# Turning the keys of batches 1 to 3 on VectorE, from loads in 16 pieces

## The chip, the cores and the metric

The kernel runs on one core of a Trainium2 chip. The metric is the device time of one execution in microseconds (us), median of several runs. A separate profiled execution gives the durations that are quoted here.

## The reference

Two blocks, one after the other. The first is a linear attention with a polynomial sketch of features; the second is a two-layer perceptron with exact Gelu on its output.

```python
batch, n_heads, seq, head_dim = (4, 4, 1088, 32); r = 8
def phi(x):                                  # S1, S2: (8, 32)
    a = np.einsum('rd,bhsd->bhsr', S1, x)
    b = np.einsum('rd,bhsd->bhsr', S2, x)
    return np.einsum('bhsi,bhsj->bhsij', a, b).reshape(*x.shape[:-1], r * r)
q_p, k_p = (phi(q), phi(k))
kv = np.einsum('bhsf,bhsd->bhfd', k_p, v)
z = np.sum(k_p, axis=2)
num = np.einsum('bhsf,bhfd->bhsd', q_p, kv)
den = np.einsum('bhsf,bhf->bhs', q_p, z)[..., None] + 1e-06
attn = num / den                             # -> x: (4352, 128), heads side by side
h = x @ w_in                                 # (4352, 2048)
g = 0.5 * h * (1.0 + erf(h / sqrt(2)))
out = g @ w_out                              # (4352, 128)
```

S1, S2, w_in and w_out arrive as 64-bit floats and are rounded to 32 bits on the chip.

## The kernel before, in words

Of the 1088 tokens of a batch, 1024 are "main" and 64 "remainder". The main tokens of the four batches make eight chunks of 512, and the remainders of all four make a ninth of 256. For each chunk n and each of 16 slices fi of the hidden width, `hidden(n, fi)` multiplies x (transposed, in xT) by a 128x128 block of w_in (L466), ScalarE applies Gelu (L468), and `project(n, fi)` adds the product with a block of w_out into o_ps (L481, L478 for the last chunk). These 144 steps are TensorE's main work. Step t runs hidden(t), then what was put in slot t, then project(t - 2). Chunks 0 and 1 share the first 32 steps, and chunks 2 and 3, of batch 1, follow from step 32.

The attention of later batches is put in slots between these steps. For batch b, with t the first step of its first chunk (32, 64, 96):

- slot t-20: `widen_v` and `widen_v_rem` copy v on GpSimd into v_aug and v_rem_aug, beside columns of ones (L278, L286).
- slot t-18: the keys are turned, so that the 32 head dimensions lie on partitions. `turn_keys` calls `key_turn(b, r, work_bank(), by_dve)` for r = 0, 1, each with four 128x128 TensorE transposes into a PSUM bank (in `transposed`, L265), and VectorE copies the bank to kT (L267).
- slot t-17: `features` calls `key_features`: 32 small matmuls per r against the sketches S12 (L303), ScalarE copies of one factor (L316), VectorE products (L317) into k_p.
- slots t-16 and t-15, for batch 1 only: `key_turn_rem` and `key_features_rem` do the same for the remainders of batches 1 and 3 (k_rem, kT_rem, k_p_rem).
- slot t-14: `finish_keys` sums k_p times v_aug over the tokens (`kv_sum`, L336; `kv_sum_rem`, L343) and takes the sum out. Slot t-13 turns that 128x128 result (L352).
- slots t-13, t-12, t-8 of each chunk: queries turned on VectorE (`query_turn`, L367), expanded (L376, L397), attended (L417, L424, L428), giving xT.

In slots 4 to 21 the rest of the weights is rounded, on VectorE and ScalarE (L209 to L239). Batch 0 is done ahead of the steps, with TensorE transposes of its own.

Which token lies where is set by the load. `load_main` (L95) puts token p*8 + j of each head on partition p at place j, in one transfer per tensor and batch with runs of 1 KB. Since kv sums over all tokens, any order will do for k and v as long as k_p and v_aug meet with the same token. `load_q` (L105) loads the queries of later chunks in four pieces of 32 partitions per chunk, so that VectorE's block transposes give the wanted order. All loads and most stores are issued by SP in the order of the text. `load_rest` issues, after the first part, the rest of the weights, then for b = 1, 2, 3 the keys, values and queries, with the remainders (k_rem, v_rem, L108) after batch 1's queries, and q_rem at the end.

The instructions of each engine run in the order of the text; a loop at the end of the kernel pins that order. PSUM tiles w_ps come from the pool wps, which has two buffers; kT has two buffers.

Of the kernel before, what the change touches and what calls it, by code (L numbers as in the profile page):

```python
# [8 lines left out]
FP = mybir.dt.float32  # L9
# [7 lines left out]
def kernel(  # L17
# [18 lines left out]
    pe, dve, act, pool, sp = nc.tensor, nc.vector, nc.scalar, nc.gpsimd, nc.sync  # L36
    B, H, S, D = q.shape
# [7 lines left out]
    MAIN = J * 128  # L45
    REM = S - MAIN
    JC = 4
    CW = JC * 128
# [9 lines left out]
    att = ctx.enter_context(tc.tile_pool(name="att", bufs=2))  # L58
# [5 lines left out]
    def work_banks():  # L64

        return wps.tile([128, 2, CW], FP, name="w_ps")

    def work_bank():
        return work_banks()[:, 0]
# [11 lines left out]
    by_act, by_dve, by_pool = act.copy, dve.tensor_copy, pool.tensor_copy  # L81
# [5 lines left out]
    main = {(n, b): big.tile([128, H, J, D], FP, name=f"{n}_{b}") for n in "kv" for b in range(B)}  # L87
# [6 lines left out]
    def load_main(eng, n, b, heads=slice(0, H)):  # L94
        eng.dma_start(out=main[n, b][:, heads],  # L95
                      in_=src_of[n][b, heads, 0:MAIN, :].rearrange("h (p j) d -> p h j d", j=J))

    def load_q(n):
        at = n % NCH * CW
        if n < NCH:  # L100
            sp.dma_start(out=q_sb[n], in_=q[0, :, at:at + CW, :].rearrange("h (p j) d -> p h j d", j=JC))
            return
        src = q[n // NCH, :, at:at + CW, :].rearrange("h (t g j) d -> g t h (j d)", g=G, j=JC)
        for g in range(G):
            sp.dma_start(out=q_sb[n][g * 32:(g + 1) * 32].rearrange("t h j d -> t h (j d)"), in_=src[g])  # L105

    def load_rem(n, b):
        sp.dma_start(out=rem[n][b // 2 * REM:(b // 2 + 1) * REM, b % 2],  # L108
                     in_=src_of[n][b, :, MAIN:S, :].rearrange("h p d -> p h d"))
# [12 lines left out]
    def load_w_in(i, gated=False):  # L122
        src, e = words(moe_w_in)
        c0, c1 = pieces[i]
        to = landing(w_in_sb[i], e == 2)
        if gated:

            pool.memset(to[0:1, 0:1], 0)
        sp.dma_start(out=to, in_=src[:, c0 * e:c1 * e])

    def load_w_out(i):
        src, e = words(moe_w_out)
        sp.dma_start(
            out=landing(w_out_sb[i], e == 2).rearrange("p (fo d) -> p fo d", d=d_model * e),
            in_=src[slice(*pieces[i]), :].rearrange("(fo fi) d -> fi fo d", fi=128))

    S_dst = landing(SR, S1.dtype != FP)
    for i, s in enumerate((S1, S2)):
        s, e = words(s)
        act.dma_start(out=S_dst[i * R:(i + 1) * R, :].rearrange("r (h d) -> r h d", h=H),  # L140
                      in_=s[:, None, :].broadcast_to([R, H, e * D]))
    nc.scalar.preload_act_table_set("gelu_and_others")
    for r in range(2):
        load_main(sp, "k", 0, slice(r, H, 2))
    load_q(0)
    load_main(sp, "v", 0)
    load_rem("k", 0)
    load_rem("k", 2)
    load_w_in(0)
    load_rem("v", 0)  # L150
    load_q(1)
    load_w_in(1)
    load_w_out(0)
    load_w_out(1)

    def load_rest():

        for i in range(2, len(pieces)):
            load_w_in(i, gated=i == 2)
            load_w_out(i)  # L160
        for b in range(1, B):
            for n in "kv":
                load_main(sp, n, b)
            for c in range(NCH):
                load_q(b * NCH + c)
            if b == 1:
                for n, b1 in (("k", 1), ("k", 3), ("v", 1), ("v", 2), ("v", 3)):
                    load_rem(n, b1)
        for b in range(B):
            load_rem("q", b)  # L170
# [90 lines left out]
    def transposed(ps, name, srcs, copy):  # L261

        n = len(srcs) * 128
        for i, s in enumerate(srcs):
            pe.transpose(ps[:, i * 128:(i + 1) * 128], in_=s, identity=ident)  # L265
        t = att.tile([128, CW], FP, name=name, bufs=3 if name == "xT" else 2)
        copy(out=t[:, :n], in_=ps[:, :n])  # L267
        return t

    def four_tokens(n, b, h, c):  # L270
        return main[n, b][:, h, c * JC:(c + 1) * JC, :].rearrange("p j d -> p (j d)")


    kT, k_p, k_p_rem, kv_T = {}, {}, {}, {}
# [13 lines left out]
    def key_turn(b, r, ps, copy):  # L288
        kT[r] = transposed(ps, "kT", [four_tokens("k", b, h, c) for h in (r, r + 2) for c in range(NCH)], copy)

    def spread(out, a, b):

        n = a.shape[1]
        return dict(out=out, in0=a[:, :, :, None].broadcast_to([128, n, R, R]),
                    in1=b[:, :, None, :].broadcast_to([128, n, R, R]))

    def key_features(b, r, banks, by_pool=()):

        for i in range(2 * NCH):
            for c in range(2):  # L300
                for t in range(2):
                    at = i * 128 + c * 64
                    pe.matmul(banks[t][c * 64:(c + 1) * 64, i * 32:(i + 1) * 32],  # L303
                              lhsT=kT[r][t * 64:(t + 1) * 64, at:at + 64],
                              rhs=S12[t * 64:(t + 1) * 64, 2 * t:2 * t + 2].rearrange("p h r -> p (h r)"),
                              start=True, stop=True)

        k_p[b, r] = att.tile([128, 2, J, R, R], FP, name="k_p")
        a = att.tile([128, 2, J, 2 * R], FP, name="a_t")
        for t in (1, 0):  # L310
            ab = banks[t][:, :128].rearrange("p (n r) -> p n r", r=2 * R)
            if t in by_pool:
                act.copy(out=a[:, t], in_=ab)
                pool.tensor_mul(**spread(k_p[b, r][:, t], a[:, t, :, 0:R], a[:, t, :, R:2 * R]))
            else:
                act.copy(out=a[:, t, :, 0:R], in_=ab[:, :, 0:R])  # L316
                dve.tensor_mul(**spread(k_p[b, r][:, t], a[:, t, :, 0:R], ab[:, :, R:2 * R]))  # L317
# [5 lines left out]
    def key_features_rem(pair, ps):  # L323
        pe.matmul(ps[:, 384:448], lhsT=kT["rem"][:, :128], rhs=S12.rearrange("p h r -> p (h r)"), start=True, stop=True)
        k_p_rem[pair] = big.tile([128, H, R, R], FP, name=f"k_p_rem{pair}")
        ab = ps[:, 384:448].rearrange("p (h r) -> p h r", r=2 * R)
        a = att.tile([128, H, R], FP, name="a_rem")
        act.copy(out=a, in_=ab[:, :, 0:R])
        dve.tensor_mul(**spread(k_p_rem[pair], a, ab[:, :, R:2 * R]))

    def kv_sum(b, ps, r):

        for i in range(J):
            ch, t, one = i // 4, i // 2 % 2, i % 2
            for c in range(NP):
                pe.matmul(ps[c * 64:(c + 1) * 64, r * F:(r + 1) * F], lhsT=v_aug[:, 2 * c + r, i, :],  # L336
                          rhs=k_p[b, r][:, t, c * 4 + ch * 2 + one].rearrange("p i j -> p (i j)"),
                          start=(r == 0 and i == 0), stop=False, skip_group_check=True)
# [12 lines left out]
    def turn_kv(b, ps, copy):  # L351
        pe.transpose(ps[:, :128], in_=kv_T[b], identity=ident)  # L352
        copy(out=kz[b].rearrange("p c n -> p (c n)"), in_=ps[:, :128])
# [158 lines left out]
    r = Rounding(SR)  # L512
# [20 lines left out]
    expand_multiply(0, 0)  # L533
    kv_bank = out_bank()
    kv_sum(0, kv_bank, 0)
    expand_copy(0, 2)
    key_features_rem(0, banks[1])
    expand_copy(0, 3)
    expand_multiply(0, 1)
    kv_sum(0, kv_bank, 1)  # L540
    kv_sum_rem(0, kv_bank)
    w_in[0].exponents()
# [7 lines left out]
    w_in[0].low_words()  # L550
    w_in[0].mantissas(by_pool=True)
    load_rest()
    w_in[0].product(pool)
    w_in[1].low_words()
# [26 lines left out]
    def at(t, f, *a):  # L581
        slots[t].append(lambda: f(*a))

    def turn_keys(b, r):
        key_turn(b, r, work_bank(), by_dve)

    def features(b, r):
        key_features(b, r, halves(work_banks()))
# [10 lines left out]
    def finish_keys(b):  # L599
        held["kv"] = work_bank()  # L600
        for r in range(2):
            kv_sum(b, held["kv"], r)
        kv_sum_rem(b, held["kv"])
        take_kv(b, held["kv"], by_dve)
# [15 lines left out]
    for b in range(1, B):  # L620
        t = NCH * b * NF
        for r in range(2):
            at(t - 20, widen_v, b, r)
        at(t - 20, widen_v_rem, b)
        for r in range(2):
            at(t - 18, turn_keys, b, r)
        for r in range(2):
            at(t - 17, features, b, r)
        if b == 1:
            at(t - 16, turn_keys_rem, b)  # L630
            at(t - 15, features_rem, b)
        at(t - 14, finish_keys, b)
        at(t - 13, lambda b=b: turn_kv(b, held["kv"], by_dve))
    for n in range(2, NCHUNK):
        t = n * NF
# [59 lines left out]
```

## Time and profile before

| | |
|---|---|
| median of 11 runs | 294.17 us (293.59 to 296.1) |
| the profiled execution | 293.96 us, span 291.6 us |
| PE (TensorE) busy | 282.3 us (97%) |
| DVE (VectorE) busy | 120.7 us (41%) |
| ACT (ScalarE) busy | 135.1 us (46%) |
| POOL (GpSimd) busy | 15.1 us (5%) |
| DMA packets | 32561, 13.37 MB |

The span is the time from the first to the last profiled instruction. The chain that ended last is followed back from the last instruction, at each step to what released it, so its shares add up to the span. PE is a matmul and PEld the load of its weights, which overlaps other matmuls; neighbouring matmuls overlap as well, so the durations of a row add up to more than the time that they take. Step 14 begins at 45.1 us, and step 32 is chunk 2's first.

### The profile page before, as it was taken

What the parts mean: (1) busy time and instruction counts of PE and PEld (TensorE: products, weight loads), DVE (VectorE), ACT (ScalarE), POOL (GpSimd) and SP (SyncE); (2) the same over time, 40 slices, a digit from 0 to 9 for tenths busy, and PEclk for the clock granted to TensorE, in tenths of its full rate; (3) what the DMA queues carried; (4) which work ended last, traced back from release to release, by engine and by line L of the source; (5) the groups of instructions that cost most, each with busy time, mean ns of one, the idle gap of its engine ahead of it and who ended that gap; (6) DMA issues with size and microseconds to landing.
All of it is one profiled execution on the core that took longest, in us unless ns stands there. A gap on an engine that the chain in (4) does not pass through costs nothing.

```text
span 291.6 us, 3792 instructions
## 1 busy us (share of the span) xinstructions
PE 282.3 (97%) x1497; PEld 137.1 (47%) x1497; DVE 120.7 (41%) x186; ACT 135.1 (46%) x259; POOL 15.1 (5%) x45
## 2 busy tenths in 40 slices
PE   7887999999999999999999999999999999999994
PEld 5633445643443345543443345533443344444694
DVE  6985686343813184251713085242513161221000
ACT  4673774265435442265335533256336533443341
POOL 3340200200000000300000000000000000000000
PEclk9999999999999999999999999999999999999999
DMA  7569587000012000200002000200001000200010
GB/s 217 160 203 370 102 231 215 7 0 0 2 28 34 11 0 2 36 2 0 0 0 37 0 2 0 39 0 0 0 9 29 0 0 0 36 2 0 9 29 18
DMA packets 32561, 13.37 MB, mean 46 GB/s; under 512 B 21408, under 2 KB 31904, under 8 KB 32544
## 3 DMA queue, kind: packets, MB, share of 16 engines
q1 hardware_dynamic: 32304, 13.05, 17.4%
q8 instruction: 12, 0.20, 0.2%
q10 hardware_dynamic: 240, 0.08, 0.1%
q14 instruction: 5, 0.04, 0.0%
HBM read 10.90 MB, written 2.23 MB: 45 GB/s over the span
## 4 chain that ended last, share of the span: by engine, by line
PE 91%; DVE 5%; issue 1%; ACT 1%; DMA 1%; ACTq 0%; DVEq 0%
PE h_ps L466 39%; PE o_ps L481 38%; PE o_ps L478 2%; PE w_ps L376 2%; PE w_ps L417 2%; PE w_ps L336 2%; DVE q_pT L397 1%; PE w_ps L265 1%; PE w_ps L303 1%; DMA raw_SR<-in_S_dram 1%; DVE k_p L317 1%; DVE bits_a L215 1%; DVE bits_e L234 0%; DVE bits_m L229 0%; PE h_ps L442 0%
## 5 line engine op out<-in xcount | busy, mean ns | idle before, releaser
L468 ACT ACTIVATE g<-h_ps 128x512 f32<-128x512 f32 (+1 forms) x144 | 82.5, 574 | 130.2 <-PE h_ps L466 129.9
L466 PE MATMUL h_ps<-xT,w_in 128*128 128x512 f32 (+1 forms) x288 | 140.3, 569 | 1.5 <-POOL w_in L239 0.8
L481 PE MATMUL o_ps<-g,w_out 128*128 128x512 f32 x256 | 133.1, 601 | 0.2 <-POOL w_out L239 0.2
L466 PEld LDWEIGHTS h_ps<-xT,w_in 128*128 128x128 f32 x288 | 53.5, 190 | 63.9 <-issue 60.3
L481 PEld LDWEIGHTS o_ps<-g,w_out 128*128 128x128 f32 x256 | 46.2, 190 | 58.1 <-issue 56.5
L424 DVE RECIPROCAL den<-den 128x512 f32<-128x512 f32 (+1 forms) x7 | 21.9, 3124 | 44.1 <-ACT den L423 44.1
L397 DVE TENSOR_TENSOR q_pT<-A_sb,w_ps 64x512 f32<-64x512 f32 x32 | 22.1, 691 | 25.4 <-ACT A_sb L383 24.8
L491 DVE STREAM_TRANSPOSE oT<-o_ps 128x512 f32<-128x512 f32 x8 | 5.7, 717 | 43.9 <-PE o_ps L481 43.9
L383 ACT COPY A_sb<-w_ps 64x512 f32<-64x512 f32 (+1 forms) x36 | 17.7, 556 | 3.1 <-PE w_ps L376 3.0
L428 DVE TENSOR_TENSOR xT<-w_ps,den 32x512 f32<-32x512 f32 (+1 forms) x28 | 18.2, 649 | 1.0
L423 ACT ACTIVATE den<-w_ps 32x512 f32<-32x512 f32 (+1 forms) x28 | 15.6, 558 | 3.0 <-PE w_ps L417 2.7
L317 DVE TENSOR_TENSOR k_p<-a_t,w_ps 128x512 f32<-128x512 f32 x12 | 8.0, 687 | 6.5 <-ACT a_t L316 6.5
L478 PEld LDWEIGHTS o_ps<-w_out,g 128*128 128x128 f32 x64 | 9.3, 191 | 0.7
L278 POOL COPY v_aug<-v 128x512 f32<-128x512 f32 x8 | 4.9, 619 | 90.6 <-issue 62.0
L478 PE MATMUL o_ps<-w_out,g 128*128 128x128 f32 x64 | 9.4, 274 | 0.0
L376 PE MATMUL w_ps<-qT,Srep 32*128 32x512 f32 x64 | 9.1, 640 | 0.0
L229 DVE SCALAR_TENSOR_TENSOR bits_m<-bits_a,bits_low 128x512 f32<-128x512 uint32 (+2 forms) x10 | 5.7, 573 | 3.7 <-ACT bits_low L209 3.1
L417 PE MATMUL w_ps<-q_pT,kz 64*64 64x512 f32 (+1 forms) x80 | 7.2, 458 | 0.0
L221 ACT ACTIVATE bits_r<-bits_e,below 128x512 uint32<-128x512 uint32 (+2 forms) x11 | 6.7, 610 | 0.6 <-DVE bits_e L213 0.5
L336 PEld LDWEIGHTS w_ps<-k_p,v_aug 128*64 128x64 f32 x192 | 5.8, 138 | 2.3 <-issue 2.3
L336 PE MATMUL w_ps<-k_p,v_aug 128*64 128x64 f32 x192 | 6.3, 224 | 0.0
L267 DVE COPY kT<-w_ps 128x512 f32<-128x512 f32 x6 | 3.9, 685 | 4.5 <-PE w_ps L265 4.5
(119 smaller groups left out, 113.3 us busy)
## 6 DMA issues: line engine op xcount, KB each, us to landing
v<-in_v_dram SPq DMA_DIRECT2D x4, 512.0 KB, 5.4
raw_w_in<-in_moe_w_in_dram SPq DMA_DIRECT2D x3, 512.0 KB, 4.6
raw_w_out<-in_moe_w_out_dram SPq DMA_DIRECT2D x3, 512.0 KB, 7.4
k<-in_k_dram SPq DMA_DIRECT2D x3, 512.0 KB, 4.8
q<-in_q_dram SPq DMA_DIRECT2D x24, 64.0 KB, 4.6
out_dram<-oT SPq DMA_DIRECT2D x24, 64.0 KB, 2.2
k<-in_k_dram SPq DMA_DIRECT2D x2, 256.0 KB, 2.9
q<-in_q_dram SPq DMA_DIRECT2D x2, 256.0 KB, 3.4
```

The source lines that it names most:

```text
L336: pe.matmul(ps[c * 64:(c + 1) * 64, r * F:(r + 1) * F], lhsT=v_aug[:, 2 * c + r, i, :], rhs=k_p[b, r][:, t, c * 4 + ch * 2 + one].rearrang ...
L376: pe.matmul(B_of[n][g // 2][:, g % 2, :W], lhsT=Srep[rows].rearrange("p a i j -> p (a i j)"), rhs=qT[n][rows].rearrange("p h j t -> p (h j ...
L383: act.copy(out=A[g // 2][F:, g % 2, :width[n]], in_=B_of[n][g // 2][:F, g % 2, :width[n]])
L397: dve.tensor_mul(out=cols[r * F:(r + 1) * F], in0=a[:, :, r::2], in1=b[:, :, r::2])
L417: pe.matmul(banks[r][c * F:(c + 1) * F, c0:c1], lhsT=kz[b][r * F:(r + 1) * F, c, :], rhs=qp[n][r * F:(r + 1) * F, c, c0:c1], start=True, s ...
L423: act.activation(out=den[h * D:(h + 1) * D, :W], in_=banks[r][at:at + D, :W], func=ACT.Copy, bias=1e-6)
L424: dve.reciprocal(out=den[:, :W], in_=den[:, :W])
L428: dve.tensor_mul(out=xT[n][rows, :W], in0=banks[h % 2][rows, :W], in1=den[rows, :W])
L466: pe.matmul(ps[:, :W], lhsT=w_tile(w_in_sb, fi), rhs=xT[n][:, :W], start=True, stop=True)
L468: act.activation(out=g_of[n, fi][:, :W], in_=ps[:, :W], func=ACT.Gelu)
L478: pe.matmul(o_of[n][:, i * 128:(i + 1) * 128], lhsT=g[:, i * 128:(i + 1) * 128], rhs=w_tile(w_out_sb, fi), start=(first and i == 0), stop= ...
L481: pe.matmul(o_of[n], lhsT=w_tile(w_out_sb, fi), rhs=g, start=first, stop=final)
```

## The change

The keys of batches 1 to 3 are loaded by `load_turned_k`, in 16 transfers a batch: one for each head h and each group pb of 32 partitions. Each brings 32 partitions times four runs of 256 bytes (two tokens). On the partition group pb, the partition t holds tokens jj*256 + t*8 + pb*2 + jc of the head, jj from 0 to 3 and jc 0 or 1. In slot t-18 `key_turn_blocks` replaces `turn_keys`: VectorE transposes 32x32 blocks, 128x256 elements per instruction, two instructions per r, straight from the loaded keys to kT, with no TensorE transpose, no PSUM bank and no copy. `kv_sum` picks the factors of k_p in the order that fits v's tokens. Batch 0, the remainders, values and queries are as before.

```diff
+    def load_turned_k(b):
+
+        src = k[b, :, 0:MAIN, :].rearrange("h (jj t pb jc) d -> h pb t jj (jc d)", jj=4, t=32, pb=4)
+        for h in range(H):
+            for pb in range(4):
+                sp.dma_start(out=main["k", b][pb * 32:(pb + 1) * 32, h].rearrange("t (jj jc) d -> t jj (jc d)", jj=4),
+                             in_=src[h, pb])
...
         for b in range(1, B):
-            for n in "kv":
-                load_main(sp, n, b)
+            load_turned_k(b)
+            load_main(sp, "v", b)
             for c in range(NCH):
                 load_q(b * NCH + c)
...
+    def key_turn_blocks(b, r):
+
+        kT[r] = att.tile([128, CW], FP, name="kT")
+        for i in range(2):
+            dve.transpose(out=kT[r][:, i * 256:(i + 1) * 256].rearrange("p (jc jj t) -> p jj jc t", jc=2, jj=4),
+                          in_=main["k", b][:, r + 2 * i].rearrange("p (jj jc) d -> p jj jc d", jj=4))
...
-            ch, t, one = i // 4, i // 2 % 2, i % 2
+
+            ch, t, one = (i % 2, i // 4, i // 2 % 2) if b else (i // 4, i // 2 % 2, i % 2)
...
-    def turn_keys(b, r):
-        key_turn(b, r, work_bank(), by_dve)
...
         for r in range(2):
-            at(t - 18, turn_keys, b, r)
+            at(t - 18, key_turn_blocks, b, r)
```

## The prediction

> **What bounds the kernel now.** I read the page first: busy time and the chain that ended last.
>
> ```profile
> PE 282.3 (97%) x1497; PEld 137.1 (47%) x1497; DVE 120.7 (41%) x186; ACT 135.1 (46%) x259; POOL 15.1 (5%) x45
> ...
> PE 91%; DVE 5%; issue 1%; ACT 1%; DMA 1%; ACTq 0%; DVEq 0%
> ```
>
> TensorE (PE) is busy throughout and holds 91% of the chain; VectorE (DVE) is busy 41% of the span. So TensorE time taken off the chain shortens the run, unless something else then arrives late. Next, the chain in order of time, around the key work of batch 1 and of batch 3 (columns: start, length, piece):
>
> ```profile
> 45.09 0.86 PE h_ps L466 x2
> 45.95 0.87 PE w_ps L265 x8
> 46.82 0.86 PE o_ps L481 x2
> 47.68 0.86 PE h_ps L466 x2
> 48.54 1.07 PE w_ps L303 x64
> ...
> 174.62 0.86 PE h_ps L466 x2
> 175.48 0.87 PE w_ps L265 x8
> 176.35 0.86 PE o_ps L481 x2
> ```
>
> The eight transposes (L265) of a batch stand on the chain with nothing beside them: hidden(14) ends at 45.95, they take 0.87 us, and project(12) follows without a gap. Batch 2 has the same piece at 110.88 us, also 0.87. There is no change of tile shape around them to pay for: L481 takes 0.86 after them as elsewhere, while after the 64-row matmuls of L303 it takes 1.05. Third, the groups by form, for prices (busy us, mean ns), and VectorE's timeline ahead of batch 1's keys:
>
> ```profile
> L265 PE MATMUL w_ps<-ident,k 128*128 128x128 f32 x24 | 3.1, 272 | 0.0
> L267 DVE COPY kT<-w_ps 128x512 f32<-128x512 f32 x6 | 3.9, 685 | 4.5 <-PE w_ps L265 4.5
> L367 DVE STREAM_TRANSPOSE qT<-q 128x512 f32<-128x512 f32 x7 | 4.9, 707 | 0.1
> L367 DVE STREAM_TRANSPOSE qT_rem<-q_rem 128x256 f32<-128x256 f32 x1 | 0.4, 448 | 0.0
> ```
>
> ```profile
> 46.23 0.69 DVE L239 TENSOR_TENSOR w_in<-bits_m,bits_e 128x512 f32<-128x512 f32 x1
> 46.84 1.28 DVE L267 COPY kT<-w_ps 128x512 f32<-128x512 f32 x2
> ```
>
> The last two rows (start, length) matter: in batch 1 VectorE is still rounding w_in when the keys' turn comes, and the kT copies start only when it is free, at 46.84. In batches 2 and 3 it idles 2.24 us until the PE transposes are done. Last, the SP queue (start, length of the issues, count):
>
> ```profile
> 18.98 1.11 SPq L95 DMA_DIRECT2D k<-in_k_dram  x1
> 20.13 2.41 SPq L95 DMA_DIRECT2D v<-in_v_dram  x1
> 22.58 8.63 SPq L105 DMA_DIRECT2D q<-in_q_dram  x8
> 31.25 1.27 SPq L108 DMA_DIRECT2D k_rem<-in_k_dram  x2
> 32.56 1.93 SPq L108 DMA_DIRECT2D v_rem<-in_v_dram  x3
> 34.54 1.28 SPq L95 DMA_DIRECT2D k<-in_k_dram  x1
> ```
>
> Eight q transfers took 8.63 us while weights were still landing, and 5.17 and 5.01 us for batches 2 and 3: 1.08 us each under load, 0.63 us each after. The queue's own waits show why: L105 waits on landings of v, k, w_out and w_in, so only a limited number of transfers is in flight.
>
> **What the Trainium skill says.** "VectorE: DVE Perf Modes", The three transpose paths: VectorE turns 32x32 blocks only and writes SBUF, TensorE does a full 128x128 into PSUM. "TensorE: Matmul & The Clock Gate", Part 4, gives about 275 ns for a PE transpose in a kernel's context; the trace has 272 as the duration, but eight in a row cost the chain 0.87 us, 0.109 each, because they overlap. "Vector Engine (DVE) Microarchitecture Reference", 3.8: the transpose is pipelined at one element per cycle per lane; the trace agrees in that 256 more columns cost 707 - 448 = 259 ns. "DMA: Bandwidth & Descriptors", Specifications, asks for at least 512 B per run for line rate; the keys go from 1 KB runs to 256 B. No view here prices those runs.
>
> **The change, part by part.**
>
> *Removed from TensorE:* 24 transposes, 3 x 0.87 = **2.6 us** of chain. It is all of it: the L303 matmuls keep their count, shapes and place. The reordered indices in kv_sum change addresses only, 0. Six PSUM tiles fewer from the two-deep w_ps pool: two fewer per batch keeps the rotation's parity, and the earlier users (chunk 1's attend and turn, or an attend six slots before) are long done; 0, and since nothing on TensorE waits for these banks now, no gain either.
>
> *VectorE:* two copies (1.28 us) become four block transposes of 128x256. Duration 448 ns each by the qT_rem row, which reads blocks in a permuted order too. For the step from one to the next I take the 512-column form: qT starts at 59.81 and the next instruction at 60.43, a step of 0.62 for a duration of 0.70; scaled, 0.448 - 0.09 = 0.36. Four: 3 x 0.36 + 0.45 = 1.53 us, 0.25 more per batch. Each also waits for four transfers on different semaphores; the trace has four separate EVENT_SEMAPHORE entries at L367 of median 35 ns, so three per transpose, 12 x 0.035 = 0.42 us at most, nothing if they pass while an earlier instruction runs. The blocks are written with gaps; that form is not in the trace, and I take no surcharge (bound: 0 to 0.1 us each; a gain below the contiguous form is excluded by the rate of one column per ns).
>
> *Batches 2 and 3:* VectorE ends the xT products at 109.12 and 173.7, then has nothing; the keys have long landed. The four transposes are done by 111 and 175.7, and L303 comes at 112.6 and 177.2 at the earliest (counted as if nothing was gained before). No wait; full 0.87 each. If that cover were gone, a wait would cost up to 1.5.
>
> *Batch 1:* L303 now comes at 48.54 - 0.87 = 47.67. VectorE's start stays 46.84, since the rounding ahead of it doesn't depend on the keys. kT[0] is ready at 46.84 + 0.36 + 0.45 = 47.65, about in time; kT[1] at 46.84 + 1.53 = 48.37. L303's first half ends at 47.67 + 0.53 = 48.20, so the second waits 0.17 us, with 0.1 for the signal 0.27. With the semaphore entries in series this becomes 0.27 + 0.42 = 0.69; with 0.1 per transpose, at most the whole 0.87. I take **0.4** lost, so 0.47 gained. Queued behind that wait are project(13) and all later matmuls, and ScalarE's Gelus behind them; nothing overtakes.
>
> *SP queue:* the keys of a batch go from one issue to 16, 45 more in all. Batch 1: eight under load at 1.08 us, to 27.6, eight at 0.63, to 32.7, against one that ended at 20.1. v is issued at 32.7 instead of 20.13, q ends near 38.3, k_rem near 39.6 instead of 32.5, v_rem near 41.5. By their landing times (v 5.4 us, k_rem 2.2, v_rem 3.3) they are there at 38.1, 41.8 and 44.8. Needs: keys on VectorE at 46.84 (landed by about 35); k_rem on TensorE at 51.4 - 0.87 = 50.5; v, through GpSimd's 1.16 us copy, by 54.4; v_rem by 56. The tightest margin is **8.7 us**; cost 0. Batches 2 and 3 add 16 x 0.63 = 10 us each, so the loads end near 50.3 + 7 + 9.4 + 9.4 = 76 us instead of 50.3. Their first user is GpSimd's v_aug copy for batch 2 (56.45 today, needed at 119.9). SP's first store is issued at 80.85, having waited 30.5 us for its data; it keeps some 5 us, and no matmul waits for it soon. The weights are ahead of the keys in the queue and don't move.
>
> **Sum.** -0.87 x 3 + 0.4 = -2.2 us. The profiled execution took 293.96 us (span 291.6 and 2.36 around it), 0.21 under the median 294.17; the profiled run goes to 291.75, the median to **292.0**. Bounds: no wait in batch 1, -2.6, 291.6; batch 1 worth nothing, -1.74, 292.4. A measurement of this kernel can tell about 0.3% (0.9 us) from no change; all of that lies beyond it.
>
> **Rivals.**
>
> *A, VectorE becomes batch 1's bound:* each strided write or its waits cost so much that L303 waits longer than the transposes took. If a transpose cost 0.75 us rather than 0.36, kT[1] would be ready at 49.9 and L303's second half wait 1.7 us; batches 2 and 3 still gain: -1.74 + 0.8 = -0.9, 293.2, about the line between faster and same. Against it: VectorE turns the like-shaped qT_rem in 448 ns. Chance 0.06.
>
> *B, the loads come late (the other side):* short 256 B runs land slowly, the limit on transfers in flight throttles the queue, and k_rem or v of batch 1 arrives after its use. It decides from where 16 key issues take 8.7 us longer than my 13.7, that is above 1.4 us each on average; every 0.1 us more per issue then puts 1.6 us on TensorE. At 1.7 us each, 4.8 us late: 294.17 - 2.2 + 4.8 = 296.8. For it: the page calls 21408 of 32561 packets under 512 B already, and 1.08 us under load is not far from 1.4. Against it: the bytes are the same, and a q transfer with twice the bytes in as many rows goes at 0.63 us once the weights are in. Chance 0.08.
>
> *C, the change doesn't do what it says:* a part of the transposes' time stays on TensorE, because the gap is filled by a wait in every batch, or the 0.87 is hidden in the modelled ends of matmuls. Then 293.5 to 294.3. Against it: starts, not ends, are 0.87 apart. Chance 0.04.
>
> **How the numbers follow.** My forecast has 0.82, its lines being 291.6 to 292.4 and 0.2 of scatter to each side. Faster: 0.82 and most of A, 0.86. Same: the rest of A, C and B at its threshold, 0.06. Slower: 0.08, B. The range goes from 291.3 (forecast's lower bound less scatter) to 293.1, which takes in most of A; B and C stay out.
>
> **What would show it.** In the changed profile: no L265 rows with k and ident in w_ps (k_rem stays); four 128x256 STREAM_TRANSPOSE writing kT per batch, near 450 ns; in the chain hidden(14), project(12), hidden(15) and L303 in a row, with a gap of 0.2 to 0.7 us at batch 1's L303 alone, released by VectorE; SP's k issues ending near 33 us, loads near 76. It would be wrong if the transposes take 600 ns or more, if TensorE waits for k_rem, v_aug or v_rem_aug near 50 us, or if batches 2 and 3 show a gap at L303.

## The result, and the profile after

The changed kernel takes 291.67 us (median of 12 runs, 291.38 to 293.69) against 294.09 us for the kernel before (47 runs): 2.42 us less, a ratio of 0.9914 with a 95% interval of 0.9896 to 0.9932. The profiled execution took 291.48 us, its span 289.2. Most line numbers of the changed kernel are 8 to 16 higher: L265 is now L273, L303 is L318, L466 is L482, L481 is L497; some experiments add 2 to 5 more. Some executions take about 2 us longer than the rest (8 of the 47, 1 of the 12), and two of the profiles below, of the loads in 32 transfers, lost 1.6 and 2.1 us in their first 16 us, so stages are compared by distances along the chain and not by their absolute starts.

The busy times and the chain's shares on the page of the changed kernel:

```profile
PE 280.2 (97%) x1473; PEld 135.0 (47%) x1473; DVE 121.7 (42%) x192; ACT 135.0 (47%) x259; POOL 16.3 (6%) x45
...
PE 92%; DVE 3%; ACT 2%; issue 1%; ACTq 0%
```

TensorE has 24 instructions and 2.1 us of busy time less, VectorE six instructions and 1.0 us more. The bound is the same. The chain in order of time (start, length, piece), first around batch 1's keys, then around batch 3's:

```profile
45.13 0.86 PE h_ps L482 x2
45.99 0.86 PE o_ps L497 x2
46.84 0.86 PE h_ps L482 x2
47.70 1.08 PE w_ps L318 x64
48.78 1.06 PE o_ps L497 x2
...
174.64 0.86 PE h_ps L482 x2
175.50 1.07 PE w_ps L318 x64
176.57 1.05 PE o_ps L497 x2
```

The piece with eight transposes is gone and its place is closed. In the kernel before, the same chain had batch 3's key features here:

```profile
178.07 1.07 PE w_ps L303 x64
```

From hidden(14) of batch 1 to the key features of batch 3 it was 178.07 - 45.09 = 132.98 us before; it is 175.50 - 45.13 = 130.37 now. That is 2.61 us, three times 0.87, with nothing lost on the way: batch 1's L318 takes 1.08 us where it took 1.07. VectorE's turn of batch 1, in its timeline, and the groups by form that price it (busy us, mean ns):

```profile
46.27 0.69 DVE L247 TENSOR_TENSOR w_in<-bits_m,bits_e 128x512 f32<-128x512 f32 x1
46.88 1.42 DVE L303 STREAM_TRANSPOSE kT<-k 128x256 f32<-128x256 f32 x4
```

```profile
L303 DVE STREAM_TRANSPOSE kT<-k 128x256 f32<-128x256 f32 x12 | 4.3, 412 | 0.0
L383 DVE STREAM_TRANSPOSE qT_rem<-q_rem 128x256 f32<-128x256 f32 x1 | 0.4, 446 | 0.0
```

Four transposes take 1.42 us: the first 0.44 us, each further one 0.33 us more. They follow the rounding as closely as the copies did before (46.84). The SP queue (start, length of the issues, count):

```profile
19.06 12.97 SPq L103 DMA_DIRECT2D k<-in_k_dram  x16
32.07 0.43 SPq L95 DMA_DIRECT2D v<-in_v_dram  x1
32.55 4.92 SPq L113 DMA_DIRECT2D q<-in_q_dram  x8
37.51 1.26 SPq L116 DMA_DIRECT2D k_rem<-in_k_dram  x2
...
40.80 7.74 SPq L103 DMA_DIRECT2D k<-in_k_dram  x16
...
66.58 2.59 SPq L116 DMA_DIRECT2D q_rem<-in_q_dram  x4
```

The issues of batch 1's keys take 12.97 us, at first while the weights land, and those of batch 2's 7.74 us, 0.81 and 0.48 each. The key loads of 32 KB, in runs of 256 bytes, land 1.8 us after their issue (median of 48). The issues of all loads end at 69.2 us. No instruction of TensorE waits for any of them.

### The profile page after: what moved, and what is told of

Read it like the earlier page. It is cut to its first block, busy times and chain, and to the rows that moved or that the text cites. A ratio compares the mean times of both kernels' runs of the same rounds, so it can differ in the third digit from the quotient of the medians.

```text
span 289.2 us, 3812 instructions
## 1 busy us (share of the span) xinstructions
PE 280.2 (97%) x1473; PEld 135.0 (47%) x1473; DVE 121.7 (42%) x192; ACT 135.0 (47%) x259; POOL 16.3 (6%) x45
## 4 chain that ended last, share of the span: by engine, by line
PE 92%; DVE 3%; ACT 2%; issue 1%; ACTq 0%
PE h_ps L482 39%; PE o_ps L497 39%; PE w_ps L392 3%; PE o_ps L494 2%; PE w_ps L433 2%; PE w_ps L352 2%; ACT A_sb L399 1%; PE w_ps L318 1%; PE w_ps L525 1%; DVE q_pT L413 1%; PE h_ps L273 1%; PE h_ps L458 0%; DVE bits_e L242 0%; ACT bits_r L229 0%; DVE bits_m L237 0%
## 5 line engine op out<-in xcount | busy, mean ns | idle before, releaser
L482 PE MATMUL h_ps<-xT,w_in 128*128 128x512 f32 (+1 forms) x288 | 140.3, 569 | 1.5 <-POOL w_in L247 0.8
L497 PE MATMUL o_ps<-g,w_out 128*128 128x512 f32 x256 | 133.1, 601 | 0.2 <-POOL w_out L247 0.2
L482 PEld LDWEIGHTS h_ps<-xT,w_in 128*128 128x128 f32 x288 | 53.5, 190 | 63.9 <-issue 60.3
L497 PEld LDWEIGHTS o_ps<-g,w_out 128*128 128x128 f32 x256 | 46.4, 190 | 59.6 <-issue 58.0
```

The costliest lines, as they stand in the source:

```text
L482: pe.matmul(ps[:, :W], lhsT=w_tile(w_in_sb, fi), rhs=xT[n][:, :W], start=True, stop=True)
L497: pe.matmul(o_of[n], lhsT=w_tile(w_out_sb, fi), rhs=g, start=first, stop=final)
```

## The experiments

Three questions were open: whether each batch's transposes are worth what they take on the chain; why batch 1 lost nothing on VectorE; and how far the loads may slip.

### One batch left as it was

```diff
-            load_turned_k(b)
+            load_main(sp, "k", b) if b == 1 else load_turned_k(b)
...
-            ch, t, one = (i % 2, i // 4, i // 2 % 2) if b else (i // 4, i // 2 % 2, i % 2)
+            ch, t, one = (i % 2, i // 4, i // 2 % 2) if b > 1 else (i // 4, i // 2 % 2, i % 2)
...
+    def turn_keys(b, r):
+        if b == 1:
+            key_turn(b, r, work_bank(), by_dve)
+        else:
+            key_turn_blocks(b, r)
...
-            at(t - 18, key_turn_blocks, b, r)
+            at(t - 18, turn_keys, b, r)
```

> Batch 1 loads and turns its keys as before; batches 2 and 3 as changed. Theory A (each batch's eight transposes are worth their 0.86 us of chain, batch 1 too): two thirds of the gain, 294.1 - 1.7 = 292.4 us, and the eight transposes back on the chain in batch 1 alone. Theory B (the prediction: batch 1 gains only 0.5 because its turn waits for VectorE): 0.5 us slower than the changed kernel, 292.1 us. The chain in order of time tells them apart: L318 of batch 3 should start 0.86 us (A) or 0.5 us (B) later than in the changed kernel.

Measured: 292.29 us (ratio to before 0.9927, 0.9903 to 0.9952). The chain of this run:

```profile
45.01 0.86 PE h_ps L482 x2
45.86 0.87 PE w_ps L273 x8
46.74 0.86 PE o_ps L497 x2
...
176.24 1.07 PE w_ps L318 x64
```

From hidden(14) to batch 3's L318 it is 131.23 us, 0.86 more than with all three batches changed, so batch 1 gives its whole 0.86 and theory A holds. The medians are 0.62 apart, nearer to B's 0.5 than to A's 0.86; they can't tell the two apart at this size, the chain can.

### The loads alone

```diff
-            ch, t, one = (i % 2, i // 4, i // 2 % 2) if b else (i // 4, i // 2 % 2, i % 2)
+            ch, t, one = i // 4, i // 2 % 2, i % 2
...
+    def turn_keys(b, r):
+        key_turn(b, r, work_bank(), by_dve)
...
-            at(t - 18, key_turn_blocks, b, r)
+            at(t - 18, turn_keys, b, r)
```

> The 16 loads a batch stay, but the keys of batches 1 to 3 are turned by TensorE and copied as before; in these batches keys meet the values of other tokens, at the same cost. Theory A (the loads are hidden, the gain is all in the transposes): the time of the kernel before, 294.1 us within 0.3, with SP's loads ending near 69 us as in the changed kernel. Rival (the new loads themselves help or hurt, for instance by easing DMA contention with the weights): 293.5 or less, or 294.7 or more.

Measured: 294.35 us, ratio 1.0019 (0.9996 to 1.0041), which holds 1. SP's loads ended at 70.1 us. The chain of this run:

```profile
44.89 0.86 PE h_ps L482 x2
45.75 0.87 PE w_ps L273 x8
...
177.87 1.07 PE w_ps L318 x64
```

The eight transposes stand on the chain again, and from hidden(14) to batch 3's L318 it is 177.87 - 44.89 = 132.98 us, as in the kernel before. The 48 small loads change nothing there, and by the interval no more than 0.4% of the whole; the gain is all in the transposes.

### More work for VectorE

```diff
-        for i in range(2):
+        for i in (0, 1) * 2:
             dve.transpose(out=kT[r][:, i * 256:(i + 1) * 256]...
```

A second kernel has `(0, 1) * 4` here.

> Each r's two block transposes of a key batch are done twice, into the same place: eight instead of four, 1.33 us more of VectorE per batch. Theory A (VectorE's time is free where it idles before L318, which is in batches 2 and 3, and has no slack at all in batch 1): batch 1 loses about 1.1 us on the chain, batches 2 and 3 nothing; 291.7 + 1.1 = 292.8 us. Rival 1 (VectorE's time is hidden everywhere): 291.7 us. Rival 2 (it costs in each batch): 291.7 + 3.5 = 295.2 us.

Measured: 292.89 us (ratio to before 0.9960, 0.9938 to 0.9981), 1.2 above the changed kernel. VectorE's key turn of batch 1 in this run, then TensorE's timeline, with the idle time before a group and who ended it:

```profile
46.97 2.72 DVE L303 STREAM_TRANSPOSE kT<-k 128x256 f32<-128x256 f32 x8
```

```profile
46.77 1.02 PE L482 MATMUL h_ps<-xT,w_in 128*128 128x512 f32 x2
48.20 0.67 PE L318 MATMUL w_ps<-S,kT 64*64 64x32 f32 x32 [0.41 <-DVE kT L303]
49.51 0.67 PE L318 MATMUL w_ps<-S,kT 64*64 64x32 f32 x32 [0.64 <-DVE kT L303]
50.11 1.12 PE L497 MATMUL o_ps<-g,w_out 128*128 128x512 f32 x2
```

From hidden(15) to project(13) it is 3.34 us, against 48.71 - 46.68 = 2.03 in the changed kernel's TensorE timeline: 1.31 lost for 2.72 - 1.42 = 1.30 more VectorE time. Batches 2 and 3 kept their 1.06 us pieces at L318. So VectorE has no slack to speak of in batch 1, and at least 1.3 us in the others.

> The same four times: sixteen transposes a batch, 4.0 us more of VectorE per batch. Theory A (a wait is what is left over the cover: some 0 us of cover in batch 1, some 2.8 us in batches 2 and 3): batch 1 loses 3.8 us, batches 2 and 3 lose 1.2 us each; 291.7 + 6.2 = 297.9 us. Rival (all of it hidden in batches 2 and 3): 295.5 us. Rival (nothing hidden): 303.7 us.

Measured: 300.34 us (ratio 1.0203, 1.0157 to 1.0249), 2.4 more than theory A. The waits were nearly as it says: counted as above, 3.93 us in batch 1 for 3.91 more VectorE time, and 1.3 us in each of batches 2 and 3 (3.33 and 3.32 us instead of 2.01 and 2.02), whose cover is then 3.9 - 1.3 = 2.6 us. The rest comes after the wait, in batch 1 (TensorE's timeline, then two stretches of the span: start and end, length, busy time and count of PE, PEld, DVE, ACT and POOL, granted clock, DMA share, GB/s):

```profile
49.54 0.67 PE L318 MATMUL w_ps<-S,kT 64*64 64x32 f32 x32 [1.72 <-DVE kT L303]
52.16 0.67 PE L318 MATMUL w_ps<-S,kT 64*64 64x32 f32 x32 [1.94 <-DVE kT L303]
52.76 2.07 PE L497 MATMUL o_ps<-g,w_out 128*128 128x512 f32 x2
54.62 1.77 PE L482 MATMUL h_ps<-xT,w_in 128*128 128x512 f32 x2
56.23 0.27 PE L273 MATMUL w_ps<-ident,k_rem 128*128 128x128 f32 x1
```

```profile
52.70:56.20 3.50, 3.50 (x14) 1.42 (x7) 2.18 (x4) 0.54 (x3) 0.00 (x0) 0.51 0.58 132
56.20:62.00 5.80, 5.80 (x76) 3.58 (x76) 0.71 (x2) 1.87 (x4) 0.61 (x1) 1.00 0.27 61
```

Two gaps of 1.72 and 1.94 us were followed by 3.5 us at a granted clock of 0.51. The steps from L497 to L482 and on to L273 took 1.86 and 1.61 us instead of 0.97 and 0.85, which is 1.65 us on top of the waits: 3.93 + 1.65 + 2.6 = 8.2 us, against 299.83 - 291.48 = 8.35 between the profiled executions. The Trainium skill's "TensorE: Matmul & The Clock Gate", Part 1, says that the clock halves after an idle window of about 3.4 us; here two gaps, neither of that length, with 32 records of small matmuls (0.67 us) between them went before the slow stretch. In batches 2 and 3 one gap of 1.1 us left the clock at 1.00.

### Which half a matmul waits for

```diff
-        for i in range(2):
+        for i in (1, 0):
             dve.transpose(out=kT[r][:, i * 256:(i + 1) * 256]...
```

> Per r, the block transposes of the second half of kT come first. In the changed kernel batch 1's L318 lost 0.01 us to VectorE instead of the predicted 0.4. Theory (each half of kT releases its own matmuls, so the matmuls of r = 1 start when the third of four transposes is done, and the fourth is finished beside them): reversed, the first matmuls of r = 1 wait for the fourth transpose, to 48.30 plus about 0.1 us for the signal, and batch 1's L318 takes some 0.3 us longer, 1.4 us; batches 2 and 3 keep 1.07. The total is 292.0 us. Rival (the matmuls wait for all of kT anyway and the transposes are simply faster than priced): L318 stays at 1.08 us.

Measured: 291.84 us (ratio 0.9909, 0.9880 to 0.9938). The chain at batch 1:

```profile
46.80 0.87 PE h_ps L482 x2
47.67 0.08 issue
47.75 1.32 PE w_ps L318 x64
49.07 1.05 PE o_ps L497 x2
```

VectorE does the same work in the same 1.42 us, from 46.84, and TensorE needs 2.27 us from hidden(15) to project(13) instead of 1.94: 0.33 lost by the order alone, at 1.06 to 1.07 us for L318 in batches 2 and 3. In the changed kernel, then, each half of kT releases its own matmuls, and the last transpose is hidden behind the three quarters of L318 that don't read it.

### How late the loads may come

```diff
-                sp.dma_start(out=main["k", b][pb * 32:(pb + 1) * 32, h].rearrange("t (jj jc) d -> t jj (jc d)", jj=4),
-                             in_=src[h, pb])
+                to = main["k", b][pb * 32:(pb + 1) * 32, h].rearrange("t (jj jc) d -> t jj (jc d)", jj=4)
+                n = 2 if b == 1 else 4
+                for j in range(0, 4, n):
+                    sp.dma_start(out=to[:, j:j + n], in_=src[h, pb][:, j:j + n])
```

A later kernel has 1 in place of the 2. A row, below, is a run of 256 bytes.

> Batch 1's keys in 32 transfers of 64 rows instead of 16 of 128; all else as in the changed kernel. Theory (late loads cost nothing until k_rem or the keys land after their use; SP's issues take 13 us for the first 16 and some 0.45 each after): the keys end near 39.5 us, k_rem is issued near 46 and lands near 48.5, two us before its use at 50.5. So 291.7 us, the same as the changed kernel. Rival (the transfers' number itself costs, in steps of some us per doubling): 294 us or more.

Measured: 292.87 us (six runs from 291.93 to 294.15, ratio 0.9952, 0.9915 to 0.9989). The median decides for neither. The profiled execution took 293.39 us, 1.91 more than that of the changed kernel, and 1.58 of it was lost ahead of hidden(15) (48.42 against 46.84). TensorE waited neither for keys nor for k_rem. But batch 1 was not free (chain, then VectorE's and GpSimd's timelines):

```profile
48.42 0.87 PE h_ps L484 x2
49.29 0.08 issue
49.37 1.32 PE w_ps L320 x64
```

```profile
47.12 1.02 DVE L244 SCALAR_TENSOR_TENSOR bits_e<-raw_w_in,bits_r 128x512 uint32<-128x512 uint32 x1 [0.54 <-ACT bits_r L231]
...
48.79 1.42 DVE L305 STREAM_TRANSPOSE kT<-k 128x256 f32<-128x256 f32 x4
```

```profile
45.93 1.67 POOL L288 COPY v_aug<-v 128x512 f32<-128x512 f32 x2 [18.66 <-PE h_ps L484]
```

L244 takes 1.02 us instead of 0.69, and everything behind it on VectorE, the key turn too, is 0.33 us late; L320 is 0.32 us longer with its gap. GpSimd's copy of v ends at 47.60 beside it, and takes 1.67 us instead of the 1.16 of the kernel before. It is late because v is: v was issued at 41.52 us, and its four loads took 4.3 to 5.8 us to land (the view names TensorE as what the copy waited for, but 41.52 + 4.3 is 45.8, where it starts). The Trainium skill's "SBUF — State Buffer", SBUF: two separate sides, says that a VectorE instruction with two SBUF inputs and a GpSimd instruction that reads SBUF exclude one another on a shared pair of ports, and that the one that starts first holds it to its end; L244 has two such inputs. The next experiment moved only v.

```diff
+            if b == 1:
+                load_main(sp, "v", b)
             load_turned_k(b)
-            load_main(sp, "v", b)
+            if b > 1:
+                load_main(sp, "v", b)
```

> As with 32 transfers for batch 1's keys, but batch 1's v is issued ahead of them. With 32 transfers L320 of batch 1 took 1.40 us instead of 1.08, and one VectorE instruction of the rounding ahead of the key turn took 1.02 us instead of 0.69 while GpSimd copied v. Theory (v came so late that GpSimd's copy fell on the stretch in which VectorE has no slack, and the two slow each other): with v early, that instruction takes 0.69 us again, the matmuls of batch 1's key features 1.08 us or less, and the time is that of the changed kernel, 291.7 us. Rival (the late keys themselves hold VectorE up): the gap of 0.3 us at the key features stays.

Measured: 291.86 us (ratio 0.9880, 0.9821 to 0.9939). The chain, VectorE and GpSimd in the same stretch:

```profile
48.94 0.86 PE h_ps L487 x2
49.80 1.08 PE w_ps L323 x64
```

```profile
47.64 0.69 DVE L247 SCALAR_TENSOR_TENSOR bits_e<-raw_w_in,bits_r 128x512 uint32<-128x512 uint32 x1 [0.55 <-ACT bits_r L234]
```

```profile
31.29 1.16 POOL L291 COPY v_aug<-v 128x512 f32<-128x512 f32 x2 [3.49 <-DMA v<-in_v_dram]
```

With v first, GpSimd copies at 31.29 us, the rounding step is back at 0.69 and the gap at the key features is gone, though the keys are issued no earlier (to 43.6 us against 41.5). So the 0.33 us came from the late v, through GpSimd's copy, and not from late keys. That a shared port is the reason is the skill's statement; the runs show the coincidence and its removal.

> Batch 1's keys in 64 transfers of 32 rows. Theory (the margin of k_rem, about 10 us, is then used up): the last keys are issued near 54 us and land near 55.5, so L318 of batch 1 waits some 7.8 us; k_rem follows near 60 and lands near 62.5, another 4 us; in all some 12 us, 303.7 us, with TensorE waiting for VectorE's kT and then for k_rem. Rival (more, smaller transfers are issued proportionally faster, so that the bytes set the time): 291.7 us.

Measured: 306.86 us, ratio 1.0425 (1.0383 to 1.0468). TensorE's timeline:

```profile
50.02 0.85 PE L320 MATMUL w_ps<-S,kT 64*64 64x32 f32 x32 [1.83 <-DVE kT L305]
57.87 0.66 PE L320 MATMUL w_ps<-S,kT 64*64 64x32 f32 x16 [6.99 <-DVE kT L305]
58.46 2.07 PE L499 MATMUL o_ps<-g,w_out 128*128 128x512 f32 x2
60.32 1.91 PE L484 MATMUL h_ps<-xT,w_in 128*128 128x512 f32 x2
63.76 0.45 PE L275 MATMUL w_ps<-ident,k_rem 128*128 128x128 f32 x1 [1.52 <-DMA k_rem<-in_k_dram]
```

The 64 issues took 36.1 us, 0.46 each once the weights were in: splitting a transfer further doesn't make its issue cheaper. TensorE waited 8.8 us for the keys and 1.5 us for k_rem, 10.3 in all; the matmuls between ran at a granted clock of 0.50. k_rem's wait is shorter than the expected 4 us because this clock made TensorE late for it: at the pace of the changed kernel, where L273 comes 1.82 us after project(13), it would have come at 60.3 and waited 3.5 us (an estimate). Of the 14.8 us between the profiled executions (306.28 - 291.48), 9.6 lie from hidden(15) to project(13) (11.65 us instead of 2.03) and 5.1 from there to the sum L354 (10.76 us instead of 5.69), of which 1.5 is the wait for k_rem and 3.6 the slow clock.

## Why the prediction was right

Point by point, by its own steps.

*The chain without the transposes:* said 2.6, measured 2.61 on the chain and 2.42 in the medians. Nothing else on TensorE moved. The span shrank by 2.4 us, though the last copy (ACT, oT) starts 2.58 us earlier, at 285.34 instead of 287.92; the missing 0.2 us lies after it, in the last stores. From that copy's start to the end of the span it is 3.7 us in the profile before, 3.9 in the changed kernel's and 3.8 to 3.9 in those of all eight experiments, the loads alone (3.9) with its old transposes among them. So the change of the transposes isn't what adds it; its cause stays open.

*VectorE's price:* said 1.53 us for four transposes, measured 1.42. The 448 ns of the single qT_rem row fit the first one (0.44); the step to the next was 0.33 and not 0.36. There was no surcharge for writing in pieces, and no time for semaphore entries (0.42 us in the upper bound): the four follow the rounding, and one another, without a gap.

*Batch 1's wait, the term that was mis-sized:* said 0.4, measured 0.01; the gap of 0.2 to 0.7 us at batch 1's L303, which was to show it, isn't there. Its start was right (46.84, measured 46.88), its end nearly (48.37, measured 48.30). The error was to let the matmuls of r = 1 wait for all of kT[1], which made 0.27 of the 0.4; the rest was an allowance for semaphores and a surcharge, and neither came. The matmuls wait for the half that they read, as the reversed order showed: there 0.33 was lost. By the prediction's own prices the third transpose ends at 46.84 + 2 x 0.36 + 0.45 = 48.01, and with 0.1 for the signal that is before 48.20, so halves give no wait. That the total came within 0.3 us is luck in part: the chain gained 0.4 more than forecast, and 0.2 of that didn't reach the total.

*Batches 2 and 3:* no wait, as said. Their cover was tested: twice the transposes cost nothing, four times cost 1.3 us each, which makes it 2.6 us.

*The loads:* said 32.7, 38.3, 39.6 and 41.5 us for the ends of the issues of keys and q, and for k_rem and v_rem; the queue shows 32.0, 37.5, 38.8 and 40.8. For batches 2 and 3 I took 0.63 us for an issue, after the q rows; it was 0.48 to 0.52, and the loads ended at 69 us, not 76. The short runs of 256 bytes, for which the prediction had no price, cost nothing that shows on the chain.

*The rivals:* A (VectorE slow) needed 0.75 us for a transpose, and it was 0.33. Its mechanism is real: 1.30 us more on VectorE cost 1.31 in batch 1. B (late loads) was right in kind and wrong in place. The transfers that come late first, at four times the number, are the keys themselves (8.8 us), then k_rem (1.5); and the first harm, at twice the number, is none of these but v, through GpSimd's copy. C is excluded by the chain and by the loads alone.

## What to carry to other kernels

A piece that stands alone on the chain of the engine that is the bound was worth its length there (0.87 us for eight transposes), not its sum of durations (8 x 272 ns). Moving it to another engine was free where that engine idles ahead of the first use; where it is busy up to that moment, count by the part that each consumer reads, and produce the parts in the order in which they are read. Before splitting a load, follow every transfer behind it on the queue, and ask too what the late data's first reader will run beside.

## What was not expected of the hardware

- Two TensorE gaps under 2 us, with 64x32 matmuls between them, were followed by 3.5 us at half the granted clock (0.51), so 3.93 us of waiting cost 5.6. Gaps of 0.41 and 0.64 us in batch 1, with twice the transposes, were followed by 3.9 us at 1.00.
- GpSimd's two 128x512 copies of v took 1.16 us in the kernel before and 1.68 in the changed one, where VectorE worked beside them, and VectorE's instructions with one input were the ones that lengthened there: L221 and L223, from 36.58 us on, took 0.83 us each, and 0.42 the next time, at 40.20. It cost nothing, since VectorE had time to make up: the key turn starts 46.88 - 45.13 = 1.75 us after hidden(14), as it did before (46.84 - 45.09). With 32 loads the same copies fell later, one instruction with two inputs took 1.02 instead of 0.69, and there it cost 0.33.
- Once the weights were in, an issue by SP with 32 rows took as long as one with 128 (0.46 and 0.48 us).
